# Late steps of a recurrent attention: k for the state from the near products through DRAM, and small TensorE work in two places of a step

## The chip, the cores and the metric

The kernel runs on one core of one Trainium2 chip. The metric is the device time of one execution in microseconds. Three runs of the kernel before took 628.48, 628.6 and 628.8 us, with a median of 628.6. The profile is of one execution of 628.35 us; its span, from the first to the last recorded instruction, is 626.6 us.

## The reference

Two blocks follow each other. The first is a linear attention with decay, over 4 batches, 8 heads, 768 tokens and 48 dimensions:

```python
state = zeros(B, H, D, D)
for t in range(S):
    cur = outer(u * k[t], v[t])
    y[t] = r[t] @ (state + cur)
    state = w[t][:, None] * state + outer(k[t], v[t])
```

The second takes the 3072 rows of 384 numbers that result, and computes

```python
h = x @ w_in                            # 384 -> 2048
sp = maximum(h, 0) + log1p(exp(-abs(h)))  # softplus
out = (h * erf(sp)) @ w_out             # 2048 -> 384
```

All of it is in float32 on the chip.

## The kernel before

**Tiling.** A step handles 128 tokens of two batches (`NJ` = 2), so of 16 pairs of batch and head (`NH`), which lie as 8 columns (`JP`) times two halves of the partitions (`e`). There are 12 steps, counted from 0: two groups of batches for each of six stretches of tokens. Inside a step the 128 tokens are two halves (`h`) of 64.

**The attention of a step.** The products of r and k between tokens of a half are found in six levels: at level n, blocks of 2^n tokens are cut in two, and r of the later half is multiplied with k of the earlier one, each scaled by products of w up to the cut. `scale` (line 235, VectorE) multiplies r and k in place in the tile `in`, level by level; the products of w are the totals `tot_sb` (line 287, GpSimd). The level products are the matmuls of line 423, and their results go to the tile `own` (line 442 on VectorE at level 5, line 449 on ScalarE at level 6).

From step 4 (`DIRECT`) on, only the upper levels use TensorE. The products within a block of 16 tokens (`NEAR`; 8 in step 4) are the near products: for each distance n from 0 to 15, r of a token is multiplied with k of the token n earlier (line 338), k is multiplied with one more w, so that it is carried on by one token (line 340), and the 48 products are summed (line 328). VectorE multiplies for distances 1 to 4, GpSimd for 5 to 15, VectorE sums all. The sums are rearranged from blocks to tokens by a write to DRAM (`by_blocks`) and a read (`by_tokens`), and line 375 puts them into `own`.

Then the output of the step gathers in the PSUM tile `y`: `from_own` (line 468) multiplies `own` with v in two calls, with `swap` 1 and 0; the state products (line 535) multiply r with the state at the start of each half (`S`, and `middle` for the second half). For the state itself k must have tokens on the partitions: `transpose` (line 479, eight of 128 x 128) and a copy by ScalarE to `kT` (line 483), then the matmuls of line 501, and on GpSimd and VectorE the decay and the sum (`faded` lines 485 and 517, `middle` line 513, `S_next` line 521).

**The second block.** `hidden` (line 584, 96 recorded matmuls a step) makes h, ScalarE copies it and takes softplus and erf, VectorE multiplies (line 573), and `project` (line 607, 64 recorded matmuls a step) makes the output. `hidden` runs one step after the attention, `project` three steps after it.

**Order.** The instructions of each engine stand in the order in which the program emits them (`manual_schedule`). `attend(s)` emits a step; at numbered places it calls `place(n)`, which emits pieces of the second block, in steps from 4 on by the strings of `in_order`: P is four matmuls of `project`, H six of `hidden`, A the next activation or multiplication. `attend(s)` also runs `prepare(s + 1)`, a generator that stops at each `yield`: totals, near products, the first scalings of the next step. So TensorE meets small attention work in four places of a late step, with P and H between them: level 5, behind the state products of the step before; level 6; `from_own(1)` with the transposes; the products into the state with `from_own(0)`.

**Buffers.** The tile `in` (r, k and w of a step) has two buffers. `load_step(s + 2)` is emitted behind the state products of step s, and the queue of SyncE, which issues most transfers in order, has the three transfers of `xT` (the step's output, for the second block) ahead of it. The GpSimd queue has, for a step: the totals of the next step, which wait for this load, then its near products, then `faded`.

Of the kernel before, what the change touches and what calls it, by code (L numbers as in the profile page):

```python
# [17 lines left out]
P = 128  # L18
EP = 64
HC = 64  # L20
NC = 2
NJ = 2
FG = 8
FT = 2

# [18 lines left out]
def view(ap, offset, dims):  # L44

    return bass.AP(ap.tensor, ap.offset + offset, [ap.ap[0], *dims])
# [12 lines left out]
def kernel(  # L59
# [47 lines left out]
    middles = [const.tile([P, JP, D], FP32, name=f"middle_{n}") for n in range(2)]  # L107
    faded = [const.tile([P, JP, D], FP32, name=f"faded_{n}") for n in range(NC)]
# [40 lines left out]
    def near_log(s):  # L149
        return NEAR_LOG - (s == DIRECT)  # L150
# [79 lines left out]
    def scale(s, level):  # L230

        in_t, tots = loaded[s][0], ready[s][1]
        half, nb = 1 << (level - 1), JP * C >> level
        halves = view(in_t[:, 0:2], half, [[JP * C - half, 2], [2 * half, nb], [1, half]])
        nc.vector.tensor_mul(  # L235
            halves, halves, view(tots[level - 1], 0, [[1, 2], [2, nb], [0, half]])
        )

    def prepare(s):
# [62 lines left out]
        if s == DIRECT:  # L302
            yield

        r, k, w = rows_of.pop(s)
        front = att.tile([P, 2, JP, C], FP32, name="rk1", bufs=1)
# [28 lines left out]
        def term(engine, *distances):  # L335

            for n in distances:
                engine.tensor_mul(terms[n], r[:, :, n:], k[:, :, : near - n])  # L338
                if n + 1 < near:
                    engine.tensor_mul(  # L340
                        k[:, :, : near - n - 1], k[:, :, : near - n - 1], w[:, :, n : near - 1]
                    )
# [21 lines left out]
        if near == NEAR:  # L364
            sum_up(*range(5, NEAR))
        by_blocks = dram.tile([P, NEAR, NEAR], FP32, name="by_blocks")
# [5 lines left out]
        yield  # L372
        scale(s, near_log(s))
# [9 lines left out]
    def attend(s, xT, place, behind):  # L383
# [4 lines left out]
        R, K = (in_t[:, x] for x in range(2))  # L388
        RK = in_t[:, 0:2]
        S, S_next = states[i][c % 2], states[i][1 - c % 2]  # L390
        middle = middles[s % 2]
        ends = tot.rearrange("p (n h) -> p n h", h=NC)
# [20 lines left out]
        for level in range(near_log(s) + 1 if s >= DIRECT else 1, LOG + 1):  # L413
            half = 1 << (level - 1)
            rk = made[:] if level == 1 else RK

            pp = products([P, NE, JP, HC])
            m = HC if level <= MASKED else half
            for n in range(JP):
                for s0 in range(0, C, HC):  # L420
                    for e in range(NE):
                        t0 = s0 if level <= MASKED else s0 + half
                        nc.tensor.matmul(  # L423
                            pp[s0 : s0 + m, e, n, :m],
                            lhsT=rk[rows(e), 1, n, s0 : s0 + m],
                            rhs=rk[rows(e), 0, n, t0 : t0 + m],
                            start=True,
                            stop=True,
                        )
            scale(s, level)  # L430
            keep_busy(DM, DM // 2)
            if level == 1 and s == 1:
                stay_warm()
            got = pp[:].rearrange("p e n t -> p (e n) t")
            if level == 1:
                if not s:
                    nc.vector.tensor_copy(out=first[:], in_=mask_sb[:, 0, :])
                nc.vector.tensor_mul(
                    own[:], got, first[:, None, :].to_broadcast([P, NH, HC])
                )  # L440
            elif level <= MASKED:
                nc.vector.copy_predicated(  # L442
                    rights(own[:], half),
                    rights(mask_sb[:, level - 1 : level, :].to_broadcast([P, NH, HC]), half),
                    rights(got, half),
                )
            else:
                for s0 in range(0, C, HC):
                    nc.scalar.copy(  # L449
                        own[s0 : s0 + half, :, half:], got[s0 : s0 + half, :, :half]  # L450
                    )
            if level > (NEAR_LOG if s >= DIRECT else 1):
                next(following, None)
            place(level - 1)

        def from_own(swap):  # L460
            for j in range(NJ):
                for q in range(0, NP, 2):
                    for h in range(NC):
                        e = h ^ swap
                        for p in (q, q + 1):
                            n = j * NP + p
                            t = slice(h * HC, (h + 1) * HC)
                            nc.tensor.matmul(  # L468
                                y[at(e, p), e, j, p // 2, t],
                                lhsT=vt[t, n * NE + e, :], rhs=own[t, e * JP + n, :],  # L470
                                start=swap == 1 and not j and not q, stop=True,
                                skip_group_check=True,
                            )

        last = c == n_pairs - 1
        from_own(1)
# [5 lines left out]
        kT = att.tile([P, JP, P], FP32, name="kT", bufs=1)  # L482
        nc.scalar.copy(kT[:], ps[:])
# [13 lines left out]
        for n in range(JP):  # L497
            for h in range(1 if last else NC):
                for e in range(NE):
                    t = slice(h * HC, (h + 1) * HC)  # L500
                    nc.tensor.matmul(  # L501
                        ps[h][rows(e), n, :D],
                        lhsT=kT[t, n, rows(e)],
                        rhs=vt[t, n * NE + e, :],
                        start=True,
                        stop=True,
                    )
        from_own(0)
# [7 lines left out]
        if not last:  # L516
            nc.gpsimd.tensor_mul(
                faded[1][:], middle[:], ends[:, :, 1:2].to_broadcast([P, JP, D])
            )
            for e in range(NE):  # L520
                nc.vector.tensor_add(S_next[rows(e)], faded[1][rows(e)], ps[1][rows(e), :, :D])
# [3 lines left out]

        for h, state in enumerate((S, middle)):
            if not (c or h):
                continue
            t = slice(h * HC, (h + 1) * HC)
            for j in range(NJ):  # L530
                for q in range(0, NP, 2):
                    for e in range(NE):
                        for p in (q + e, q + 1 - e):
                            n = j * NP + p
                            nc.tensor.matmul(  # L535
                                y[at(e, p), e, j, p // 2, t],
                                lhsT=state[rows(e), n, :], rhs=R[rows(e), n, t],
                                start=False, stop=True, skip_group_check=True,
                            )

        y3 = att.tile([P, UNIT], FP32, name="y3", bufs=1)
        nc.scalar.copy(y3[:].rearrange("p (j t) -> p j t", j=NJ), y[:, 1, :, 1])
        for j in range(NJ):
            nc.scalar.copy(xT[:, 0:2, j * C : (j + 1) * C], y[:, 0, j])
        nc.scalar.copy(xT[:, 2, :].rearrange("p (j t) -> p j t", j=NJ), y[:, 1, :, 0])
        for kk in range(KT):
            n = D // KT
            for e, queue in enumerate((nc.sync, nc.scalar)):
                queue.dma_start(
                    out=xT[e * EP + D : (e + 1) * EP, kk, :],  # L550
                    in_=y3[e * EP + kk * n : e * EP + (kk + 1) * n, :],
                )
# [96 lines left out]
    def in_order(s, k):  # L649


        order = ("APPPAPP", "APPPHH", "AHHH", "AHHH")
        if s == DIRECT:
            order = ("APPP", "APPP", "APPHH", "AHHH", "AHHH")
        for what in order[k]:
            if what == "A":
                advance()
            elif what == "P":
                piece(projs, s - 3)
            else:  # L660
                piece(hids, s - 1)
# [19 lines left out]
    with tc.manual_schedule(  # L681
# [5 lines left out]
        for t in (*states[0], *states[1], *middles):  # L687
            nc.gpsimd.memset(t[:], 0.0)
        nc.scalar.copy(u_row[:, :1], ident[:, :1])
# [11 lines left out]
        for s in range(n_steps):  # L701
# [8 lines left out]
            def place(n):  # L710
                if n == LOG - 1 and DIRECT - 1 <= s < n_steps - 2:
                    load_rows(s + 2)
# [15 lines left out]

            attend(s, xTs[s], place, lambda: convert_at(LOG + 2))
# [4 lines left out]
        for k in range(12):  # L734
            in_order(n_steps + k // 4, k % 4)
# [96 lines left out]
```

## Time and profile before

| | busy us | share of the span |
|---|---|---|
| TensorE (PE) | 611.9 | 98% |
| VectorE (DVE) | 402.6 | 64% |
| ScalarE (ACT) | 301.3 | 48% |
| GpSimd (POOL) | 258.0 | 41% |

| group | count | busy us |
|---|---|---|
| L584, hidden, TensorE | 1152 | 259.5 |
| L607, project, TensorE | 768 | 254.0 |
| L423, level products, TensorE, from `in` | 2368 | 38.4 |
| L479, transposes, TensorE | 96 | 13.1 |
| L483, kT copy, ScalarE | 12 | 12.2 |
| L235, scalings with totals, VectorE | 60 | 90.8 |
| L338 and L340, near terms, GpSimd, from and to `words` and `rk` | 147 | 151.9 |

The counts are recorded instructions; a wide matmul of the program stands as two. Busy time of different engines overlaps. The granted TensorE clock is 0.999 over the span.

### The profile page before, as it was taken

How to read it: one execution, taken by the hardware profiler on the slowest of the kernel's cores; microseconds unless marked ns; L12 is line 12 of the kernel's file. 1: busy time of each engine (PE TensorE's matmuls, PEld its weight loads, DVE VectorE, ACT ScalarE, POOL GpSimd, SP SyncE). 2: the span in 40 equal slices, each digit the busy share in tenths (PEclk: the TensorE clock that was granted, in tenths of full speed). 3: DMA queues.
4: the chain of work that ended last, by engine and by line, in shares of the span. 5: the costliest groups of instructions: out<-in, count | busy, mean ns of one | idle time of the engine just before them, and what ended most of it. 6: DMA issues, size and time to landing. Idle time of an engine off the chain costs nothing.

```text
span 626.6 us, 15491 instructions
## 1 busy us (share of the span) xinstructions
PE 611.9 (98%) x6886; PEld 451.0 (72%) x6886; DVE 402.6 (64%) x445; ACT 301.3 (48%) x374; POOL 258.0 (41%) x267
## 2 busy tenths in 40 slices
PE   8989999999999999999999999999999999999997
PEld 7668777578678668668668768768768768768654
DVE  5697696994597996895795796797796430020300
ACT  2547878535546534534534534534534543534600
POOL 4448184600278197096097097097087100000000
PEclk9999999999999999999999999999999999999999
DMA  8375471330320600511420421321310100000000
GB/s 330 124 267 189 182 252 56 160 110 10 134 103 9 213 29 12 175 67 18 154 82 12 157 84 18 132 103 19 115 45 10 17 14 13 7 25 1 0 26 25
DMA packets 32819, 54.83 MB, mean 88 GB/s; under 512 B 19568, under 2 KB 24944, under 8 KB 31344
## 3 DMA queue, kind: packets, MB, share of 16 engines
q1 hardware_dynamic: 31600, 53.25, 24.4%
q8 instruction: 54, 0.88, 0.6%
q10 hardware_dynamic: 1152, 0.59, 0.4%
q14 instruction: 13, 0.11, 0.1%
HBM read 46.88 MB, written 5.77 MB: 84 GB/s over the span
## 4 chain that ended last, share of the span: by engine, by line
PE 83%; DVE 8%; POOL 3%; issue 2%; ACT 2%; DMA 1%; SPq 0%; DVEq 0%; POOLq 0%; ACTq 0%
PE m L607 36%; PE m L584 34%; PE pp L423 5%; DVE in L235 3%; PE pp L479 2%; PE y L468 2%; PE y L535 2%; PE pp L501 1%; PE m L686 1%; DMA in<-in_rkw 1%; DVE sums L328 1%; POOL tot_sb L287 1%; DVE h L573 1%; DVE own L442 1%; DVE words L340 1%
## 5 line engine op out<-in xcount | busy, mean ns | idle before, releaser
L584 PE MATMUL m<-xT,w_in_sb 128*128 128x256 f32 x1152 | 259.5, 382 | 1.5 <-DVE w_in_sb L203 1.3
L607 PE MATMUL m<-w_out_sb,h 128*128 128x384 f32 x768 | 254.0, 489 | 1.3 <-POOL w_out_sb L207 1.3
L584 PEld LDWEIGHTS m<-xT,w_in_sb 128*128 128x128 f32 x1152 | 215.5, 190 | 35.2 <-issue 2.4
L607 PEld LDWEIGHTS m<-w_out_sb,h 128*128 128x128 f32 x768 | 144.0, 190 | 98.7 <-POOL w_out_sb L207 1.9
L593 ACT COPY h<-m 128x512 f32<-128x512 f32 x96 | 56.0, 583 | 133.8 <-PE m L584 133.7
L235 DVE TENSOR_TENSOR in<-in,tot_sb 128x1024 f32<-128x1024 f32 x60 | 90.8, 1514 | 41.2 <-PE pp L423 39.1
L573 DVE TENSOR_TENSOR h<-h,sp 128x1024 f32<-128x1024 f32 x48 | 70.8, 1516 | 60.7 <-ACT sp L569 60.7
L340 POOL TENSOR_TENSOR words<-words,rest 128x480 f32<-128x480 f32 (+4 forms) x70 | 72.4, 1035 | 5.5
L287 POOL TENSOR_TENSOR tot_sb<-in 128x512 f32<-128x512 f32 x12 | 15.0, 1247 | 121.3 <-DMA in<-in_rkw 121.3
L328 DVE TENSOR_REDUCE sums<-words 128x6 f32<-128x288 f32 (+8 forms) x66 | 30.4, 472 | 35.6 <-POOL words L338 35.3
L338 POOL TENSOR_TENSOR rk<-words 128x528 f32<-128x528 f32 (+3 forms) x28 | 47.9, 1712 | 6.2 <-issue 4.0
L616 ACT COPY o<-m 128x384 f32<-128x384 f32 x24 | 11.5, 478 | 79.3 <-PE m L607 79.1
L423 PEld LDWEIGHTS pp<-in 48*64 48x64 f32 (+1 forms) x2368 | 33.8, 125 | 17.4 <-issue 8.0
L566 ACT ACTIVATE sp<-h 128x2048 f32<-128x2048 f32 x24 | 45.9, 1911 | 0.3
L569 ACT ACTIVATE sp<-sp 128x2048 f32<-128x2048 f32 x24 | 45.9, 1911 | 0.3
L423 PE MATMUL pp<-in 48*64 48x64 f32 (+1 forms) x2368 | 38.4, 212 | 4.8 <-DVE in L235 2.2
L569 ACT ACT_TABLE_LOAD x24 | 30.8, 1283 | 20.5 <-issue 18.0
L287 POOL TENSOR_TENSOR tot_sb<-tot_sb 128x256 f32<-128x256 f32 (+4 forms) x60 | 35.1, 584 | 4.5
L328 DVE TENSOR_REDUCE sums<-rk 128x14 f32<-128x672 f32 (+9 forms) x54 | 34.7, 698 | 0.0
L338 POOL TENSOR_TENSOR words<-words 128x336 f32<-128x336 f32 (+6 forms) x49 | 31.6, 646 | 3.8
L566 ACT ACT_TABLE_LOAD x24 | 30.8, 1283 | 3.2 <-issue 2.8
L449 ACT COPY own<-pp 32x512 f32<-32x512 f32 x24 | 13.8, 575 | 35.5 <-PE pp L423 35.2
(67 smaller groups left out, 458.2 us busy)
## 6 DMA issues: line engine op xcount, KB each, us to landing
in<-in_rkw SPq DMA_DIRECT2D x11, 1536.0 KB, 7.0
words<-in_moe_w_in SPq DMA_DIRECT2D x8, 768.0 KB, 5.6
words<-in_moe_w_out SPq DMA_DIRECT2D x8, 768.0 KB, 4.6
words<-in_rk_rows SPq DMA_DIRECT2D x8, 768.0 KB, 8.6
v<-in_v SPq DMA_DIRECT2D x12, 384.0 KB, 7.3
out<-o SPq DMA_DIRECT2D x24, 192.0 KB, 1.9
rest<-in_w_rows SPq DMA_DIRECT2D x8, 384.0 KB, 8.7
in<-in_rkw SPq DMA_DIRECT2D x2, 512.0 KB, 4.9
```

Source lines behind the costliest of these rows:

```text
L235: nc.vector.tensor_mul(halves, halves, view(tots[level - 1], 0, [[1, 2], [2, nb], [0, half]]))
L287: nc.gpsimd.tensor_mul(new, pair[:, :, 0], pair[:, :, 1])
L328: nc.vector.tensor_reduce(out=view(sums[:], n, [[near * (NEAR + 1), NEAR // near], [NEAR + 1, near - n]]), in_=terms[n], axis=mybir.AxisLi ...
L338: engine.tensor_mul(terms[n], r[:, :, n:], k[:, :, : near - n])
L340: engine.tensor_mul(k[:, :, : near - n - 1], k[:, :, : near - n - 1], w[:, :, n : near - 1])
L423: nc.tensor.matmul(pp[s0 : s0 + m, e, n, :m], lhsT=rk[rows(e), 1, n, s0 : s0 + m], rhs=rk[rows(e), 0, n, t0 : t0 + m], start=True, stop=True,)
L566: nc.scalar.activation(held[0][:], h[:], AF.Softplus)
L569: nc.scalar.activation(held[0][:], held[0][:], AF.Erf)
L573: nc.vector.tensor_mul(h[:, part], h[:, part], held[0][:, part])
L584: nc.tensor.matmul(ps[:, ff, :], lhsT=w_in_sb[:, g * FG + f + ff, kk * P : (kk + 1) * P], rhs=xT[:, kk, :], start=kk == 0, stop=kk == KT - 1,)
L593: nc.scalar.copy(h[:, f : f + FT, :], ps[:])
L607: nc.tensor.matmul(ps[j][:], lhsT=gs[g][:, f, j * C : (j + 1) * C], rhs=w_out_sb[:, g * FG + f, :], start=g + f == 0, stop=g == NG - 1 and ...
```

## The change

From step 5 on the transposes are left out. k, which the near products carry on in place, is now carried to the end of its block of 16 (one more w per distance: `m`), so that at the end each k holds the decay from its token to the end of its block. The rows with it are written to DRAM (`k_blocks`) and read back with tokens on the partitions (`kT`). What is missing is the decay from the end of the block to the end of the half of 64: three small GpSimd operations put it together from the totals (`over_blocks`), two small matmuls turn it (`spread_blocks`), ScalarE copies it, and it goes through DRAM too, to be spread over the tokens (`g_rows`, `spread`). VectorE multiplies `kT` by it. k therefore no longer needs the scaling at level 6, and `scale` leaves it out there. The code of `attend` is split into functions, and a new `attend_late` emits steps from 5 on in another order: `from_own(1)` of the step before, level 5, `from_own(0)` and the state products of the step before stand in one place; level 6, the turning matmuls and the products into the state in the other. All P pieces stand between the first and the second, all H pieces between the second and the first of the next step. `fence`, a small VectorE copy out of `y`, stands between the two calls of `from_own`. `middle` and `faded` have one buffer each instead of two.

The purpose is to have less TensorE work that is not the two wide products, and to change between the two kinds less often.

The functions that are only moved (`level_products`, `take_level`, `from_own`, `state_part`) compute as before and are left out here.

```diff
     def scale(s, level):
...
+        n = 1 if s > DIRECT and level == LOG else 2
+        halves = view(in_t[:, 0:2], half, [[JP * C - half, n], [2 * half, nb], [1, half]])
...
+            to = over_blocks[:].rearrange("p (h b) n -> p b h n", h=NC)
+            nc.gpsimd.tensor_mul(to[:, 0], quarter, half)
+            nc.gpsimd.tensor_copy(out=to[:, 1], in_=half)
+            nc.gpsimd.tensor_copy(out=to[:, 2], in_=last)
...
                 engine.tensor_mul(terms[n], r[:, :, n:], k[:, :, : near - n])
-                if n + 1 < near:
-                    engine.tensor_mul(
-                        k[:, :, : near - n - 1], k[:, :, : near - n - 1], w[:, :, n : near - 1]
-                    )
+                m = near - n - (s == DIRECT)
+                if m:
+                    engine.tensor_mul(k[:, :, :m], k[:, :, :m], w[:, :, n : n + m])
...
         if near == NEAR:
             sum_up(*range(5, NEAR))
+            k_blocks = dram.tile([P, NEAR, D], FP32, name="k_blocks")
+            nc.sync.dma_start(out=k_blocks[:], in_=k_rows)
         by_blocks = dram.tile([P, NEAR, NEAR], FP32, name="by_blocks")
...
+            kTs[s] = att.tile([P, NH, D], FP32, name="kT", bufs=1)
+            nc.sync.dma_start(
+                out=kTs[s][:], in_=k_blocks[:].rearrange("(g b) s d -> (b s) g d", g=NH)
+            )
         scale(s, near_log(s))
...
+    def fence():
+        nc.vector.tensor_copy(
+            out=seen[:].rearrange("p (e g t) -> p e g t", e=NE, g=NP),
+            in_=y[:].rearrange("p e j q t -> p e (j q) t")[..., HC - 1 : HC + 1],
+        )
...
+    def spread_blocks(s, pp):
+        n = D // 2
+        for e in range(NE):
+            nc.tensor.matmul(
+                pp[:EP, e, 0:2, HC // 2 : HC // 2 + n],
+                lhsT=over_blocks[rows(e)].rearrange("p b n -> p (b n)"),
+                rhs=ident[rows(e), rows(e)], start=True, stop=True,
+            )
+        few = att.tile([EP, NE * 2, n], FP32, name="few", bufs=1)
+        nc.scalar.copy(
...
+        nc.sync.dma_start(
+            out=g_rows[:].rearrange("b (n d) -> (b n) d", n=JP),
...
+        nc.sync.dma_start(
+            out=spread[s][:].rearrange("p n e d -> p (n e d)"),
...
+    def attend_late(s, place):
+        c, in_t, vt, own, S, S_next, ends = parts_of(s)
+        RK = in_t[:, 0:2]
+        before = s - 1 if s - 1 > DIRECT else None
+        if before:
+            from_own(before, ready[before][0], 1)
+            fence()
+        pp = products([P, NE, JP, HC])
+        level_products(pp, RK, LOG - 1)
+        scale(s, LOG - 1)
+        take_level(own, pp, LOG - 1)
+        if before:
+            from_own(before, ready[before][0], 0)
+            through_state(before, xTs[before])
+            if s + 1 < n_steps:
+                load_step(s + 1)
+        following = prepare(s + 1) if s + 1 < n_steps else iter(())
+        kT = kTs[s]
+        nc.vector.tensor_mul(
+            kT[:].rearrange("p (e n) d -> p n e d", e=NE),
+            kT[:].rearrange("p (e n) d -> p n e d", e=NE), spread[s][:],
+        )
+        nc.gpsimd.tensor_mul(faded[0][:], S[:], ends[:, :, 0:1].to_broadcast([P, JP, D]))
+        next(following, None)
+        place(0)
+        next(following, None)
+        place(1)
+        pp = products([P, NE, JP, HC])
+        level_products(pp, RK, LOG)
+        if s + 1 < n_steps:
+            spread_blocks(s + 1, pp)
+        take_level(own, pp, LOG)
+        ps = products([P, NC, JP, HC])
+        ps = [ps[:, h] for h in range(NC)]
+        state_part(s, kT, ps)
+        scale(s, LOG)
+        for e in range(NE):
+            nc.vector.tensor_add(middle[rows(e)], faded[0][rows(e)], ps[0][rows(e), :, :D])
+        place(2)
+        next(following, None)
+        if s < n_steps - SPC:
+            nc.gpsimd.tensor_mul(
+                faded[1][:], middle[:], ends[:, :, 1:2].to_broadcast([P, JP, D])
+            )
+            for e in range(NE):
+                nc.vector.tensor_add(S_next[rows(e)], faded[1][rows(e)], ps[1][rows(e), :, :D])
+        place(3)
+        for _ in following:
+            pass
+        place(4)
...
-        order = ("APPPAPP", "APPPHH", "AHHH", "AHHH")
+        order = ("APPPAPP", "APPP", "HH", "AHHH", "AHHH", "PPAPP")
...
+        s = n_steps - 1
+        from_own(s, ready[s][0], 1)
+        fence()
+        advance()
+        piece(projs, s - 2)
+        from_own(s, ready[s][0], 0)
+        through_state(s, xTs[s])
+        in_order(s + 1, 5)
+        for k in range(1, 15):
+            in_order(s + 1 + k // 5, k % 5)
```

## The prediction

> **What bounds the kernel now.** I read the busy shares first (PE 611.9 of 626.6 us), then the chain of waits over one late step, because an average over 12 steps says nothing of the stage that is changed. In the chain below (start, duration, engine, line) each row starts where the one before ends.
>
> ```profile
> 301.65 1.04 PE y L535 x64
> 302.69 0.93 PE pp L423 x64
> 303.62 13.10 PE m L607 x40
> 316.72 0.69 PE pp L423 x50
> 317.41 7.94 PE m L607 x24
> 325.35 5.18 PE m L584 x24
> 330.52 0.59 PE y L468 x32
> 331.12 1.02 PE pp L479 x8
> 332.14 7.77 PE m L584 x36
> 339.91 0.87 PE pp L501 x64
> 340.78 0.45 PE y L468 x32
> 341.23 7.97 PE m L584 x36
> ```
>
> TensorE has no gap from one set of state products (L535) to the next: a late step is 47.55 us (302.69 to 350.24) of TensorE. So removed TensorE work is gained, as long as nothing else then becomes longer than the step.
>
> What could is the chain that prepares the next step. I took it from the timelines of GpSimd, VectorE and the DMA queue for the same step. VectorE ends it (start, duration, operation, in brackets the idle time ahead and its releaser):
>
> ```profile
> 340.14 2.85 DVE L573 TENSOR_TENSOR h<-h,sp 128x1024 f32<-128x1024 f32 x2
> 342.92 1.13 DVE L513 TENSOR_TENSOR middle<-faded,pp 48x384 f32<-48x384 f32 x2
> 344.99 1.12 DVE L521 TENSOR_TENSOR s<-faded,pp 48x384 f32<-48x384 f32 x2 [0.95 <-POOL faded L517]
> 346.14 1.23 DVE L235 TENSOR_TENSOR in<-in,tot_sb 128x1024 f32<-128x1024 f32 x1
> 347.28 1.22 DVE L375 TENSOR_TENSOR own<-block_sb,by_tokens 128x1024 f32<-128x1024 f32 x1
> 351.24 1.23 DVE L235 TENSOR_TENSOR in<-in,tot_sb 128x1024 f32<-128x1024 f32 x1 [2.74 <-PE pp L423]
> ```
>
> The scaling at 346.14 ends at 347.37; the level-5 products of the next step (L423) need it and start at 350.24. So the slack is 2.9 us of 47.55. I count this chain from E, the end of the state products (302.69): `in` is issued at 305.94, after three xT transfers that hold the DMA queue; it has landed when GpSimd starts:
>
> ```profile
> 313.18 1.04 POOL L287 TENSOR_TENSOR tot_sb<-in 128x512 f32<-128x512 f32 x1 [16.04 <-DMA in<-in_rkw]
> 314.30 2.73 POOL L287 TENSOR_TENSOR tot_sb<-tot_sb 128x256 f32<-128x256 f32 x5
> 316.99 1.33 POOL L338 TENSOR_TENSOR rk<-words 128x528 f32<-128x528 f32 x1
> ```
>
> Behind the totals in its queue stand 21 near terms, the last ending at 339.98. Over five steps (E = 255.14, 302.69, 350.24, 397.78, 445.33; last term 292.16, 339.98, 387.27, 434.42, 482.39) that end is E+37.0 in the mean, 36.6 to 37.3.
>
> **What the Trainium skill says.** "SBUF — State Buffer", section "Who interferes with whom": a VectorE instruction with two SBUF inputs and a GpSimd instruction that reads SBUF block each other for a whole instruction; reductions never do. The trace agrees: GpSimd's 480-wide term takes 1.20 us or 2.07, its faded product 0.83 or 1.81; VectorE's line 375 takes 1.22 or, beside that product, 1.86. "Trainium Architecture — The Big Picture", "Inside one NeuronCore": engines run apart and meet only in semaphores; so what counts is the order in each queue. "DMA: Bandwidth & Descriptors", "Anatomy of one DMA — SWDGE (gpsimd) path": some 2 us of a transfer are fixed, most of it the receipt of the last write. SyncE issues these here, and the trace agrees roughly: xT lands 1.8 us after issue, by_blocks 1.7, by_tokens 2.9.
>
> **The change, part by part: TensorE.** The row of the 8 transposes is 1.02 us. A run of wide products costs 215.8 ns each for L584 (20.72 us / 96 in the tail of the chain) and 322.6 for L607 (41.29 / 128). By that 36 of L584 are 7.77, as after the transposes, but 7.97 after small products; 40 and 24 of L607 are 12.90 and 7.74 against 13.10 and 7.94. So going back to wide work costs 0.20, and going into small work 0.59 - 0.45 = 0.14 (L468 after wide and after small): 0.34 for a place. The transposes pay 0.20 of that in their own row: 0.82 to 0.88 remain, I take 0.85.
> - Per late step: transposes -0.85; two places fewer -0.68; two spreading products of 48 columns +0.1 (estimate from L501's rate, between 0.03 and 0.2). TensorE's own step becomes 47.55 - 1.43 = 46.1.
> - Merging lines 535, 423 and 468 removes no product.
>
> **VectorE.** Per step: scaling at level 6 for r alone, half of 1.23; multiplying kT by the spread factors +0.95 to 1.12 (line 357 is 128x768 too); wider near terms, 192 columns, +0.2; `fence`, 128x16 out of PSUM, 0.2 (nearest 128x48 reduce 0.20; 0.1 to 0.3). VectorE is idle for about 10 us of a step, so only its place in a chain matters: the fence does stand in one.
>
> **New waits, and what is queued behind them.** `fence` waits for the own products with swap 1; behind it on VectorE stand the scaling at level 5 and the level-5 blocks, needed by level 6 some 21 us later. Multiplying kT waits for two loads; behind it stand VectorE's near terms, which GpSimd needs at E+14: some us of room. The load of kT waits on the DMA queue for the write of k_blocks, ahead of xT and `in`, but at about E+42.5, before these are due. The store of the spread factors waits for ScalarE's small copy after level 6 and holds the loads of rows for the step after next: room of half a step. Beyond the fence's own 0.2, counted below, these waits cost nothing; the work named hides them.
>
> **ScalarE.** The 1.01 us kT copy goes, a 64x96 copy comes: beside other work, 0.
>
> **DMA.** k_blocks is written and read back as kT (384 KB each way), and spread is loaded. kT is multiplied only after the fence and needed 20 us later: 0. But k_blocks is written ahead of by_blocks in one queue. by_tokens landed 4.9 us after the last term at 202.03 (by_tokens issued 204.04, + 2.9); at the 300 GB/s of the loads, k_blocks puts 1.3 on it: 6.2.
>
> **The chain, new, from E.** GpSimd: last term at 37.0; three new 16-wide operations for `over_blocks`, 0.22 + 0.08 each (48 wide is 0.29, 96 is 0.39), +0.9, ahead of the terms; k is now carried one distance further, so the widths 480..48 become 528..48, one 528 operation more, 1.33 + 0.08 = +1.4; VectorE is in contention 1 us less (half a scaling), -0.4. Last term E+38.9. Now faded[1], formerly behind middle, is the first thing behind the terms: 0.85, 39.8. S_next 1.15: 40.95. Only then h x sp, 2.85 and 0.64 for GpSimd's faded[0] beside it: 44.4. Scaling at level 4, 1.2: **45.6**; level 5 may start. own 1.15: 46.75, with by_tokens at 38.9 + 6.2 = 45.1 just in time. fence 0.2: 46.95. Behind the fence waits line 468 with swap 0 (0.45), then the state products (0.9): the next E at **48.3**.
>
> This is a loop: the state products release the buffer of the next `in`. Before, level 5 came after E, and the chain had until E+47.55. Now level 5, fence and 1.35 us of products lie ahead of the next E. The loop of 48.3 is longer than TensorE's 46.1: TensorE waits some 2.2 us in front of level 5 and swap 0, and the step is 0.75 longer than before. In step 10, without S_next, by_tokens decides: 45.1 + 1.15 + 0.2 + 1.4 = 47.85.
>
> **The sum.** Level 5 of step 5 (207.37) waits for VectorE already, behind the terms of step 4's preparation: +1.6 (1.4, and 0.2 on VectorE) = 208.97. To the next level 5: 0.16 for the cold start and 46.1 - 1.35 (the own products and state products of step 4 were earlier), then level 5 and 1.35, 2.28: E of step 5 is 256.2; the loop (206.2 + 48.3) is earlier. Four loops, steps 6 to 9: 193.2. Step 10: 47.85. E of step 10: 497.25. From level 5 of step 11 to the end the profile has 626.6 - 492.86 = 133.74; less level 5 (0.93, already done), transposes 0.85 and one place 0.35: 131.6. Span 628.85, and 2.0 between span and time (628.6 - 626.6): **630.8 us**.
>
> **Rivals.** Every us of the loop counts about five times: time = 389.35 + 5 x loop, if step 10 is 0.45 below the loop.
> - TensorE stays the bound, faster: 256.2 + 5 x 46.1 + 131.6 + 2.0 = **620.3**. For it: no gap on TensorE now, and `in` is no longer followed at once by the loads of rows, so it may land sooner than 7 us. Against: the load with no rows behind it (448.20) took 7.0 too. 2.2 us would have to vanish from the chain. Chance 0.12.
> - The loop binds, but nearer 47.3, if h x sp and faded[0] do not meet and over_blocks is cheaper: 389.35 + 236.5 = **625.9**. Chance 0.2. At 47.6 to 48.1 the time is within 0.2%.
> - by_tokens or `in` come later beside the new transfers, loop 49.0: **634.4**. Chance 0.15.
> - The forecast: 0.53.
>
> The ends of the unknown terms (fence 0.1 to 0.3, over_blocks 0.6 to 1.0, `in` at E+9.4 to 10.5, faded[0]'s 0 to 0.64) make 0.7 on the loop, 3.5 on the time; leaving out the 620 case and the far end of the slow one gives 625 to 634.5. Faster by over 0.2% (loop under 47.6): the first rival, most of the second and a little of the forecast, 0.26; within, 0.19; slower, 0.55.
>
> **What would show it.** Right: in the late steps TensorE waits 1 to 3 us for line 235's operation on VectorE or for the fence; E to E is about 48.3; the chain of waits leaves TensorE there and goes through VectorE, GpSimd and `in`; the tail after step 11's level 5 is 2 us shorter. Wrong: no wait on TensorE in steps 6 to 10 and 46.1 from E to E; or the waits there, but with the last term before E+38, so that the loop ends under 47.6; or TensorE waiting for kT ahead of the products into the state.

## The result, and the profile after

The changed kernel takes 636.85 us (median of four runs: 638.04, 638.04, 635.66, 634.01), against 628.6 before: 1.0124 times as long, with an interval of 1.0086 to 1.0163. The forecast was 630.8, with a range of 625 to 634.5: the direction is right, the rise is almost four times as large as forecast, and the time lies outside the range. The profiled run took 638.04 us with a span of 636.3; the forecast span was 628.85, so 7.45 us are to be found.

The page of the kernel after shows first that the clock is no longer full all through. The first line is the granted TensorE clock in 40 slices of 15.9 us, in tenths; the second the chain of waits by engine.

```profile
PEclk9999999999999799999999999799999999999999
PE 52%; POOL 22%; DVE 9%; DMA 8%; issue 5%; ACT 2%; SPq 1%; POOLq 0%; DVEq 0%; ACTq 0%
```

TensorE now carries 52% of the chain. Two slices have a 7: at about 207 to 223 and at about 398 to 414 us. The mean clock is 0.989 (before: 0.999). In the four runs it went with the time: 0.989 in the two of 638.04, 0.995 in the two of 635.66 and 634.01.

The chain over step 7 (start, duration, engine, line), from one set of state products (L484) to the next, shows the loop that the prediction drew:

```profile
306.88 0.94 PE y L484 x63
...
309.99 1.57 SPq L498
...
311.66 6.88 DMA in<-in_rkw
...
318.61 1.05 POOL tot_sb L293
...
323.28 1.22 POOL over_blocks L316
324.50 1.14 POOL over_blocks L317
...
347.13 0.80 POOL faded L587
...
349.11 3.00 DVE h L705 x2
352.11 1.15 DVE in L241
353.30 1.21 PE pp L424 x64
...
354.52 0.19 DVE seen L467
354.75 0.66 PE y L458 x32
355.42 0.94 PE y L484 x63
```

From E = 307.82 to 356.36 is 48.54 us; 48.3 were forecast. In words: state products, three xT transfers in the queue (L498), the load of `in`, totals, `over_blocks`, near terms to 347.13 (E+39.3), `faded`, S_next, h x sp, the scaling (to E+45.4), level 5, `fence` (L467, column `seen`), `from_own(0)`, state products. TensorE waits twice on it; the view of its waits has us in total, times, and the longest:

```profile
PE pp L424 <- DVE in L241: 6.6, 7, 2.2
PE y L458 <- DVE seen L467: 3.5, 4, 2.2
```

These are the forecast waits, but not in every step. Call the stretch from E5 to E6 step 6, and so on: the two waits together are 0.3 us in step 6, 1.8 in step 7 (1.52 and 0.29), 3.9 in step 8, nothing in step 9 and 0.8 in step 10, where 2.2 in each was forecast; one of 2.2 stands ahead of level 5 of step 5. What was not forecast at all follows some of them. The windows below have the stretch, its length, the busy times with counts of TensorE, its weight loads, VectorE, ScalarE and GpSimd, then the granted clock, the DMA share and GB/s; the second fence is TensorE's timeline of the waits there, with the wait and its releaser in brackets.

```profile
402.00:403.00 1.00, 0.98 (x64) 0.98 (x64) 0.00 (x0) 0.00 (x0) 0.00 (x0) 1.00 1.17 160
404.00:405.00 1.00, 0.00 (x0) 0.00 (x0) 1.00 (x1) 0.00 (x0) 0.00 (x0) 0.50 0.64 82
...
409.00:410.00 1.00, 1.00 (x3) 0.61 (x2) 0.97 (x2) 0.47 (x2) 0.00 (x0) 0.50 0.00 0
411.00:412.00 1.00, 1.00 (x5) 0.60 (x4) 0.96 (x2) 0.67 (x1) 0.00 (x0) 1.00 0.20 52
```

```profile
402.02 1.16 PE L424 MATMUL pp<-in 48*64 48x64 f32 x64 [1.71 <-DVE in L241]
405.39 1.11 PE L458 MATMUL y<-own,v 64*48 64x64 f32 x32 [2.21 <-DVE seen L467]
```

From 403.33 to 410.16 us, behind the wait of 1.71 us and through that of 2.21, the clock is half of the full one; such a stretch is called a spell of low clock below. The 32 products of L458 take 1.11 us instead of 0.66, the state products after them 1.71 instead of 0.94, the 64 of L739 21.8 instead of 20.84. The same happens from 208.77 to 215.60 us, behind the wait of 2.22 us in front of level 5 in step 5: level 5 takes 1.99 instead of 1.16, the 64 of L739 23.2.

In step 8 `own` starts late, and the transfers ahead of it show why (start, duration):

```profile
396.33 3.91 DMA by_blocks<-sums
400.26 3.63 DMA by_tokens<-by_blocks
403.91 1.24 DVE own L398
```

By step:

| | forecast | measured | difference | what it consists of |
|---|---|---|---|---|
| start to E5 | 256.2 | 260.7 | +4.5 | low clock 3.2; a gap of 1.03 inside the state products |
| E5 to E6 | 48.3 | 47.1 | -1.2 | `in` issued at E+2.9 and landed in 6.45 |
| E6 to E7 | 48.3 | 48.54 | +0.2 | |
| E7 to E8 | 48.3 | 51.85 | +3.55 | by_tokens late: waits 2.1 longer than in step 7; low clock 1.2 |
| E8 to E9 | 48.3 | 48.82 | +0.5 | no wait of the loop: TensorE's own 46.3, low clock 1.0, 1.5 around a gap of 1.23 |
| E9 to E10 | 47.85 | 47.3 | -0.55 | |
| E10 to the end | 131.6 | 132.0 | +0.4 | |

### The profile page after: what moved, and what is told of

Same layout as the page of the kernel before. It is cut to its first block, busy times and chain, and to the rows that moved or that the text cites. A ratio compares the mean times of both kernels' runs of the same rounds, so it can differ in the third digit from the quotient of the medians.

```text
span 636.3 us, 15558 instructions
## 1 busy us (share of the span) xinstructions
PE 610.9 (96%) x6858; PEld 451.3 (71%) x6858; DVE 397.0 (62%) x459; ACT 293.5 (46%) x374; POOL 278.6 (44%) x295
## 4 chain that ended last, share of the span: by engine, by line
PE 52%; POOL 22%; DVE 9%; DMA 8%; issue 5%; ACT 2%; SPq 1%; POOLq 0%; DVEq 0%; ACTq 0%
PE m L739 22%; PE m L716 21%; POOL words L358 8%; DMA in<-in_rkw 6%; PE pp L424 4%; POOL rk L354 4%; POOL tot_sb L293 4%; POOL words L354 3%; DVE in L241 2%; PE y L484 2%; PE y L458 1%; SPq L498 1%; DMA by_tokens<-by_blocks 1%; DMA by_blocks<-sums 1%; DVE h L705 1%
## 5 line engine op out<-in xcount | busy, mean ns | idle before, releaser
L739 PE MATMUL m<-w_out_sb,h 128*128 128x384 f32 x768 | 255.8, 493 | 1.3 <-POOL w_out_sb L212 1.3
L739 PEld LDWEIGHTS m<-w_out_sb,h 128*128 128x128 f32 x768 | 146.2, 192 | 101.9 <-issue 3.0
L241 DVE TENSOR_TENSOR in<-in,tot_sb 128x1024 f32<-128x1024 f32 (+1 forms) x60 | 83.4, 1391 | 38.4 <-PE pp L424 36.5
L705 DVE TENSOR_TENSOR h<-h,sp 128x1024 f32<-128x1024 f32 x48 | 66.3, 1423 | 52.4 <-ACT sp L701 52.2
L358 POOL TENSOR_TENSOR words<-words,rest 128x528 f32<-128x528 f32 (+10 forms) x77 | 72.5, 941 | 6.0
L748 ACT COPY o<-m 128x384 f32<-128x384 f32 x24 | 11.5, 480 | 119.3 <-PE m L739 119.3
L344 DVE TENSOR_REDUCE sums<-words 128x6 f32<-128x288 f32 (+8 forms) x66 | 30.4, 472 | 44.7 <-POOL words L354 44.3
L293 POOL TENSOR_TENSOR tot_sb<-tot_sb 128x256 f32<-128x256 f32 (+4 forms) x60 | 43.1, 718 | 4.5
L354 POOL TENSOR_TENSOR rk<-words 128x528 f32<-128x528 f32 (+3 forms) x28 | 40.5, 1446 | 4.7 <-issue 2.4
L344 DVE TENSOR_REDUCE sums<-rk 128x14 f32<-128x672 f32 (+9 forms) x54 | 35.5, 704 | 10.6 <-POOL rk L354 10.4
L354 POOL TENSOR_TENSOR words<-words 128x336 f32<-128x336 f32 (+6 forms) x49 | 30.3, 618 | 3.8
L358 DVE TENSOR_TENSOR words<-words,rest 128x576 f32<-128x576 f32 (+8 forms) x34 | 28.7, 845 | 1.2
```

Of the source, the lines that this page charges most:

```text
L241: nc.vector.tensor_mul(halves, halves, view(tots[level - 1], 0, [[1, n], [2, nb], [0, half]]))
L293: nc.gpsimd.tensor_mul(new, pair[:, :, 0], pair[:, :, 1])
L344: nc.vector.tensor_reduce(out=view(sums[:], n, [[near * (NEAR + 1), NEAR // near], [NEAR + 1, near - n]]), in_=terms[n], axis=mybir.AxisLi ...
L358: engine.tensor_mul(k[:, :, :m], k[:, :, :m], w[:, :, n : n + m])
L705: nc.vector.tensor_mul(h[:, part], h[:, part], held[0][:, part])
L739: nc.tensor.matmul(ps[j][:], lhsT=gs[g][:, f, j * C : (j + 1) * C], rhs=w_out_sb[:, g * FG + f, :], start=g + f == 0, stop=g == NG - 1 and ...
```

## The experiments

Three theories, with the numbers that the expectations use. **Theory 1**: the time is the loop of waits (load of `in`, GpSimd, VectorE, level 5, fence); shorten it and TensorE is the bound again. **Theory 2**: VectorE's queue alone makes the step longer, and the transfers have room. **Theory 3**: the loss is a lower TensorE clock that comes from the new order of the work and not from waits. Beside them stands a question on the low clock: under theories 1 and 2 it comes from TensorE's waits, so that a kernel whose TensorE doesn't wait long keeps the full clock. The experiments below are edits of the changed kernel but for e8; the 113 runs of the kernel before beside them took 626.8 to 631.0 us.

### e1: h x sp out of the chain

From step 5 on the multiplication h x sp of place 3 is emitted behind the multiplication of `kT` in the next step.

```diff
+        while put_off:
+            put_off.pop(0)()
...
-            if what == "A":
+            if what == "A" and k == 3 and DIRECT < s < n_steps:
+                put_off.append(later.pop(0)[0])
+            elif what == "A":
```

> The changed kernel with one thing moved: VectorE's multiplication h x sp of the second half of the units, 3.0 us, stands behind the multiplication of kT of the next step instead of ahead of the scaling at level 4. Theory 1 (a loop: state products, load of in, GpSimd's near terms, VectorE, level 5 and fence, state products): the scaling at level 4 comes 2.4 to 3 us sooner, so level 5 waits no longer; but by_tokens lands at E+45.5 in the changed kernel, so own and the fence stay where they are, TensorE waits 1.5 to 2 us in front of swap 0 instead, and the step stays at 48 to 48.5 us: 633 to 637 us. Theory 2 (VectorE's queue alone makes the step longer, the transfers have room): the step falls to 46.1 and the time to 622 to 626. Theory 3 (the loss is a lower TensorE clock that comes from the new order and not from waits): no change, 636.9, clock 0.99 or 0.995.

Measured: 635.25 us, 1.0114 [1.0095, 1.0132], clock 0.991: as theory 1 expects, and 9 us above the 622 to 626 of theory 2, which falls. TensorE's waits of this kernel:

```profile
PE y L458 <- DVE seen L467: 5.3, 5, 1.9
PE pp L424 <- DVE in L241: 3.1, 5, 2.2
```

The wait ahead of level 5 is gone in the late steps (6.6 to 3.1, and 2.2 of these are step 5), and the wait at the fence took its place (3.5 to 5.3). Behind the scaling in VectorE's queue stand `own`, which waits for by_tokens, and the fence: taking 3 us from one branch of the loop only brings out the other. The clock is at half for three spells of 3.4 us.

### e3 and e4: by_blocks ahead of k_blocks

e3 puts the write of k_blocks, 384 KB, behind the read of by_tokens in the queue; e4 has this and the edit of e1.

```diff
-            nc.sync.dma_start(out=k_blocks[:], in_=k_rows)
...
+        if near == NEAR:
+            nc.sync.dma_start(out=k_blocks[:], in_=k_rows)
```

> The changed kernel with by_blocks written and by_tokens read ahead of the write of k_blocks, VectorE's queue unchanged. Theory 1 (loop, with two chains that end nearly together): h x sp still stands ahead of the scaling at level 4, so own cannot start before E+45.5 whenever by_tokens lands; the steps keep their 48.3 to 48.5 us, and only the late by_tokens of step 8 (1.9 us) is saved: 632 to 636 us, nearer the changed kernel than e4. Rival (the transfers alone make the step longer): as e4 or better, 630 or less.

> e1 and, besides, by_blocks is written and by_tokens read ahead of the write of k_blocks. Theory 1: by_tokens now lands some 1.3 us sooner (E+44.2), own ends at 45.4, the fence at 45.6, the next E at 47.0: loop 47.0 to 47.3, so 1.2 to 1.5 us less in each of steps 6 to 9: 628 to 632 us; better than e1 by 3 to 6. Theory 2: the same as e1. Theory 3: no change against the changed kernel.

Measured: e3 633.7 us, 1.0085 [1.0066, 1.0104]; e4 630.05 us, 1.0036 [1.0018, 1.0055]. Both are in the ranges that theory 1 gave. In e3 by_blocks lands 1.7 us after its issue in every late step, where it took 2.3 behind k_blocks in four steps and 3.91 in step 8, and in step 8 `own` finds by_tokens there. The gains of e1 (1.6 us) and of e3 (3.2) are smaller than the spread of the runs, so neither edit alone is told from the changed kernel with certainty; both together gain 6.8 us, clear of it.

The profiles say less for e4 than its time does. From E5 to E10 the changed kernel takes 243.6 us, e1 241.5, e3 240.2 and e4 240.2 again; single steps of e4 take 46.8 to 49.4, where a loop of 47.0 to 47.3 was expected. Of the 5.3 us by which the span of e4 is shorter than that of e1, 4.0 lie ahead of E5, where e4 has no spell of low clock. In e4 the load of kT comes later, VectorE waits 1.4 to 1.7 us for it ahead of h x sp and its near terms, and GpSimd's last term ends at E+38.9 to E+40.5 instead of E+37.9 to E+39.5; `own` still waits for by_tokens. That the two edits remove two branches of the loop is therefore not shown by e4; e2, below, is the test of the loop. Waits at the fence of 5.9 us in five steps, the longest 2.9, are left in e4, and its runs show what the clock is worth: the three at a mean clock of 1.000 took 627.1, 627.5 and 628.9 us, two at 0.989 634.0 and 636.2. With one and the same kernel, then, 0.011 of mean clock goes with some 7 us.

### e2: the load of `in` ahead of the xT transfers

The load is emitted straight behind the state products, so it no longer stands in the queue behind the copies and transfers of xT. Nothing is left out.

```diff
-    def through_state(s, xT):
+    def through_state(s, xT, then=lambda: None):
...
+        then()
         y3 = att.tile([P, UNIT], FP32, name="y3", bufs=1)
...
-            through_state(before, xTs[before])
-            if s + 1 < n_steps:
-                load_step(s + 1)
+            through_state(
+                before, xTs[before], lambda: load_step(s + 1) if s + 1 < n_steps else None
+            )
```

> The changed kernel with the load of the next in issued directly behind the state products, ahead of the three xT transfers, which held it for 2.8 to 3.3 us. Theory 1 (loop): everything from the load to own comes 2.5 to 3 us sooner against E, by_tokens included; the loop falls from 48.5 to under 46, TensorE's 46.1 bounds the steps 6 to 10; the only wait left is that of level 5 in step 5 (2.2 us), with its spell of low clock (3 us): 623 to 627 us. Theory 2 (VectorE's queue): also faster, so this run does not tell 1 from 2. Theory 3 (clock from the new order): no change in clock; the steps get shorter by their waits alone, some 8 us in all, but spells of low clock stay in the late steps: 629 to 632.

Measured: 626.06 us over 20 runs, 0.9964 [0.9953, 0.9974]. This beats both kernels, lies in the range of theory 1, and is below the 629 to 632 of theory 3. `in` is issued at E+0.06 instead of E+2.9 to E+3.8. GpSimd's timeline in this kernel, E = 306.14:

```profile
313.50 1.06 POOL L293 TENSOR_TENSOR tot_sb<-in 128x512 f32<-128x512 f32 x1 [14.28 <-DMA in<-in_rkw]
...
317.46 0.24 POOL L316 TENSOR_TENSOR over_blocks<-tot_sb 128x16 f32<-128x16 f32 x1
317.65 0.20 POOL L317 COPY over_blocks<-tot_sb 128x16 f32<-128x16 f32 x1
```

It starts at E+7.4 instead of E+10.8, and the two operations that took 1.22 and 1.14 us take 0.24 and 0.20, since VectorE sums beside them (L344) where h x sp ran. The near terms behind them take 24.4 us instead of 21.4, as h x sp now runs beside those, and the last term ends at E+36.2 instead of E+39.3. In the chain, TensorE has no gap over the loop:

```profile
350.14 0.93 PE pp L424 x64
351.07 0.45 PE y L458 x32
351.52 0.90 PE y L484 x64
352.41 4.71 PE m L740 x14
```

E to E is 46.28 us (306.14, 352.42, 398.69), against 46.1 worked out for TensorE's own step. So the TensorE part of the prediction holds, and what withheld it was the loop. Ahead of these steps the kernel still waits 2.17 us (level 5 of step 5) and 1.94 (level 5 of step 6), and has a gap of 1.09 inside the state products; its clock stays full there.

### e5: filler products in place of waits

Two products of 128 x 384 whose result nothing uses ahead of level 5 in every late step, and one behind it from step 6 on; the rest is computed as in the changed kernel.

```diff
+    def fill(ps, times):
+        for _ in range(times):
+            nc.tensor.matmul(
+                ps[:, :DM], lhsT=ident[:], rhs=w_in_sb[:, 0, :], start=True, stop=True,
+            )
...
+        fill(pp[:, 0].rearrange("p n t -> p (n t)"), 2)
         level_products(pp, RK, LOG - 1)
...
+        if before:
+            fill(ps_m.tile([P, DM], FP32, name="m"), 1)
```

> The changed kernel with TensorE kept busy where it waits: in each step from 5 on, two additional products of 384 columns (0.65 us each) ahead of level 5 and one behind it, into PSUM that is not read; nothing is taken away from the waits of the chain. If the spells of low clock come from the waits (theories 1 and 2), they go, though no wait is shorter: clock 0.999, the 5 us that they cost in the profile come back, and the fillers cost about 2 us where TensorE had not waited that long (step 6, step 11): 632 to 635 us, and the runs lie closer together than 634.0 to 638.0. If they come from the order or length of the wide stretches (theory 3), the clock stays at 0.99 and the time rises to 638 to 640.

Measured: 639.3 us, 1.0176 [1.0155, 1.0198], clock 1.000 in the profile and 0.997 to 1.000 in the four runs. The waits ahead of level 5:

```profile
PE pp L424 <- DVE in L241: 2.2, 6, 0.7
```

With no wait over 0.83 us in the late steps the clock stays at 1.000 and every stretch of 64 of L748 (project in this kernel) takes 20.84 us. So the low clock comes from TensorE's waits and not from the order of the work, and theory 3 falls, though the time is the one that it gave. The time expected of the fillers did not come out: they take 1.5 us ahead of level 5 and about 1 behind it, which is more than they fill; from E6 on TensorE has no wait left and E to E is 48.9. Filling a wait that ends on another engine costs as soon as the filler outlasts it.

### e8: the new k, in the old order

The kernel before with its four places, k through DRAM instead of the transposes, and nothing of the new order or the fence; the product into the state reads `kT` as in the changed kernel, and `middle` and `faded` have one buffer each as there.

```diff
-    middles = [const.tile([P, JP, D], FP32, name=f"middle_{n}") for n in range(2)]
+    middle = const.tile([P, JP, D], FP32, name="middle")
...
+            if level == LOG and DIRECT <= s < n_steps - 1:
+                spread_blocks(s + 1, pp)
...
+            if s > DIRECT and level == LOG - 1:
+                kT = kTs[s]
+                nc.vector.tensor_mul(
+                    kT[:].rearrange("p (e n) d -> p n e d", e=NE),
+                    kT[:].rearrange("p (e n) d -> p n e d", e=NE), spread[s][:],
+                )
```

> One half of the change alone: from step 5 on k for the state comes through DRAM as in the changed kernel, but the small TensorE work stands in four places as before, level 5 behind the state products, h x sp ahead of middle, no fence. Theory 1 (the loss comes from the new order, which puts level 5, fence and 1.35 us of products into the loop): TensorE's step is 47.55 - 0.75 = 46.8; the longer GpSimd chain brings the scaling at level 4 from E+44.5 to E+46.8 or 47.5, where level 5 is due at 46.8, so waits of 0 to 0.7 us: 623.5 to 627.5 us, faster than before. Rival (the new route itself, GpSimd's 1.4 to 3 us and the transfers, is what is too long): waits of 1.5 to 2 us in each step and 630 or more.

Measured: 630.27 us over 20 runs, 1.0029 [1.0016, 1.0042]. The time expected under theory 1 (623.5 to 627.5) is missed, and the number is that of the rival, by another path than the rival's. No late step after step 5 waits ahead of level 5, as theory 1 has it, but there is a new wait:

```profile
PE pp L523 <- POOL over_blocks L318: 3.7, 5, 1.0
```

In the old order level 6 comes some 14 us after E, and the products that turn `over_blocks` stand right behind it; GpSimd has `over_blocks` only at about E+15.5. E to E is 47.8 (257.7, 305.5, 353.3): what the transposes leave free goes into this wait. So new k alone costs 1.7 us here (630.27 - 628.6), with a spell of low clock behind the wait of 2.16 us in step 5 among it, and the new order with the load where it was another 6.6 (636.85 - 630.27).

### e7, e9, e10, e11: the waits that e2 leaves

All four keep the edit of e2. e9 puts three fillers ahead of level 5 of step 5. e7 has the edits of e1 and e3 as well, and one P piece of step 5 moved ahead of its level 5. e10 moves the same P piece, and issues the load first in step 4 too; e11 adds the edit of e3 to e10. The edit of e10, but for that of e2:

```diff
+        if s == DIRECT + 1:
+            piece(projs, s - 3)
         level_products(pp, RK, LOG - 1)
...
-        through_state(s, xT)
+        through_state(s, xT, (lambda: load_step(s + 2)) if s == DIRECT else (lambda: None))
...
+        if s == DIRECT + 1:
+            order = ("APPAPP", *order[1:])
```

> e2 with three additional products of 384 columns (1.95 us, unread PSUM) ahead of level 5 of step 5 only, where e2 waits 2.2 us for VectorE: the one long wait is filled, at no cost in time, and nothing else is changed. If the spells of low clock follow long waits: clock 0.999 or above in every run, 623.5 to 625 us, and the spread of e2's runs (624.2 to 628.1) is gone above 625. If not: the same as e2, 626.1, and the same spread.

> e1, e2 and e3 together, and one piece of four products of project (2.6 us) moved from behind level 5 of step 5 to ahead of it, where TensorE waited 2.2 us. Theory 1: every late step is bound by TensorE at 46.3 us as in e2, the wait in step 5 is filled with work that has to be done anyway, no wait is longer than 1 us and the clock stays at 0.999 or above: 620.5 to 623.5 us, 2 to 4 us less than e2. Rival (the spells of low clock do not come from the waits): clock still 0.995 to 0.997 and 623 to 626.

> e2, with the load of in issued ahead of xT also behind the state products of step 4, and with one piece of four products of project (2.6 us) ahead of level 5 of step 5. h x sp stays where the changed kernel has it: in e7 its place behind kT made GpSimd's near terms end at E+40.1 against E+36.2 in e2. Theory 1: the two waits of e2 that are left (2.2 us in step 5, 1.9 in step 6) are gone, all late steps take TensorE's 46.3 us, and as no wait is over 1 us, there is no spell of low clock: 620.5 to 622.5 us, clock 0.999 or above, runs within 1.5 us of each other; below before and below e2. Rival (spells of low clock come without waits too): 622 to 626, with a spread as in e2.

> e10, and by_blocks and by_tokens ahead of k_blocks. With the loop no longer binding, by_tokens has some 2 us of room (own did not wait for it in e2), so nothing should change: within 1 us of e10. If it is slower, the later kT (its load now starts behind by_tokens) is waited for by VectorE, and then by the near terms.

Measured: e9 628.12 us, 0.9990 [0.9976, 1.0003]; e7 627.24 us, 0.9984 [0.9968, 0.9999]; e10 626.74 us, 0.9965 [0.9954, 0.9975]; e11 628.12 us, 0.9987 [0.9974, 0.9999]. None beats e2; e9, e7 and e10 miss their expected time by 3.1 to 4.2 us, and e11 is 1.4 above e10 where 1 was allowed. In e9 the first wait is filled and the one at step 6 stays (1.97 us), with a spell of low clock behind it; but its four runs at a mean clock of 1.000 also took 626.0 to 627.8 us, against 624.2 to 626.7 in e2, so the clock is not all that e9 loses. e10 shows why such edits bring nothing:

```profile
PE pp L424 <- DVE in L241: 5.0, 5, 4.0
```

The wait of 2.17 at step 5 is gone, and the one at step 6 grew from 1.94 to 4.04. It ends with the preparation of step 6, which started no earlier: its `in` was issued 2.4 us sooner (207.52 against 209.92), 1.0 us behind the load of kT, took 9.35 us instead of 6.7, and landed at 216.87 against 216.60. In e7 the last terms come at E+38.0 to E+40.1 instead of E+35.5 to E+36.2. The terms themselves take no longer (24.5 us in step 9, 24.4 in e2); what takes longer stands ahead of them. In step 9 VectorE waits 2.38 us for kT, whose load is later by the edit of e3, then has h x sp and its own near terms; beside these GpSimd's totals and `over_blocks` take 8.0 us instead of 4.7. So the 3 us taken out of one place of VectorE's queue were paid in another.

## Why the prediction was right or wrong

**Right: TensorE's own step.** 46.1 forecast, 46.28 in e2.

**Right: the loop, and what ends it; in part, its size.** 48.3 forecast, 48.54 in step 7; level 5 of step 5 at 208.97 forecast, 208.84 measured; the tail 131.6 against 132.0. The marks that would show it right came in part: the chain goes through VectorE, GpSimd and `in` in steps 6, 7 and 8, but waits of 1 to 3 us at level 5 or the fence stand only in steps 7 and 8. Steps 6 and 10 took 47.1 and 47.3, near the second rival, and in step 9 TensorE itself was the bound. e2 shows that this loop is what keeps the kernel from being faster: with the load earlier by 2.8 to 3.8 us, and nothing else changed, the late steps are those of the first rival. That rival's own argument, that `in` may land sooner than 7 us, held in four of the five steps (6.45 to 6.88 us, 7.93 in step 8). The 5.7 us by which e2 misses its 620.3 are 1.94 and 0.18 of waits and 1.09 of a gap ahead of E5, 0.9 for five loops, 0.7 around a gap of 0.42 in step 9, 0.3 each in the tail and between the profiled run and the median, and some 0.3 left.

**Right as a sum, wrong in its terms.** Some terms had errors that cancelled. `over_blocks`, 0.9 with an upper end of 1.0, took 2.48 us (323.28 to 325.76) beside h x sp. The page "SBUF — State Buffer", cited for exactly this, was applied to the wide operations only; this trace shows that a 16-wide one waits just as long. The totals took 4.67 us instead of 3.9, for the same reason, and `in` came at E+10.8 in step 7 instead of the mean of E+10.0. Against this, the contention fell on the early operations and not on the later terms, so that the last term came at E+39.3, for 38.9 forecast.

**Wrong in step 8: "by_tokens just in time".** At 6.2 us behind the last term it was to land as `own` can start. In step 8 it came 8.0 us behind (last term 395.86, `own` 403.91): by_blocks took 3.91 us to land and by_tokens 3.63, for the 1.7 and 2.9 of before. `own` waited 1.94 us, and TensorE 2.1 longer than in step 7. The third rival spoke of this, at 0.7 us in every step; it was some 2 in one. The write of k_blocks is the smaller part of the cause: ahead of by_blocks it costs 0.6 us (2.3 against 1.7 in e3), where 1.3 was forecast. The other 1.6 us of by_blocks in step 8 stays open; one such landing stands in e4 too, with k_blocks behind (3.05 us from 391.21), and one in the kernel before (2.88 from 340.25).

**Wrong, and the largest: "The sum".** It priced every wide product at its full rate and a wait at its own length, with 0.16 for a cold start, and put the clock at nothing. In this profile the low clock behind waits took 0.83 and 2.4 us in step 5, and 1.2 and 1.0 around E8: 5.4, of which some 4.4 moved E. The row from which the 0.16 comes, level 5 of step 5 behind a wait of 1.18 us, ran at full clock, so the profile of before didn't show this cost; the prediction didn't ask what the clock does after longer waits. That the low clock is tied to waiting rests on e5, which has no long wait in the late steps and keeps 1.000, and on where the low spells lie in all twelve profiles (last section). How much the clock costs is seen in e4's runs. The length of a wait alone doesn't decide: in e2's profile waits of 2.17 and 1.94 us passed at full clock, and one of 2.92 in e4's; in e9's a wait of 1.97 us brought a spell, and in e4's a wait of 0.52 and a gap of 1.13 did.

**Not in the prediction: gaps inside the state products**, 1.03 us in step 5 (259.31 to 260.34) and 1.23 in step 9 (454.92 to 456.15), charged to no engine or transfer. Gaps of 0.2 to 1.9 us stand in the state products of steps 5 or 9 in e1 to e5, e10 and e11 too, and none in e7, e8 and e9. In the changed kernel a transfer of the queue that the page calls "instruction" stands up to 2 us ahead of each (258 to 259 and 453 to 454 us), but one at 306 to 307 goes without a gap. No run was aimed at them; their cause stays open.

With these the difference closes: low clock 4.4, by_tokens 2.1 and the first gap 1.0 make 7.5 of the 7.45. That the rest comes to nothing is luck: +0.5 in step 9, +0.4 in the tail and some smaller ones stand against -1.2 in step 6 and -0.55 in step 10.

## What to carry to other kernels

Before TensorE work is removed from a step that is full, write the next step's preparation as a loop with its times; if it is longer than the shortened step, the gain turns into a wait, and moving the load at its head may be worth more than the edit itself (here 10.8 us). No run gives the earlier load to the kernel before, whose late steps have no wait that it could shorten. Price a new wait on TensorE above its length, since the products behind it may run at half clock for 3.4 us or more. Moving an operation out of a loop pays only if what it then runs beside or ahead of is not itself in the loop: h x sp was paid back at the fence in e1 and ahead of GpSimd's terms in e7.

## What the runs showed of the hardware

- In the clock records of the twelve profiles the granted clock is 1.00 or 0.50, and within a profile all its changes lie whole multiples of 3.413 us apart (in the changed kernel 208.77, 215.60, 403.33 and 410.16). Every profile can be divided at these points into stretches of 3.413 us. The seventeen stretches at full clock that stand ahead of a low spell have TensorE without a matmul for 44 to 75% of the time (1.5 us or more); of the 2143 others, up to 1 us before the end of the span, seven have 42 to 49%, and the rest less.
- So a wait brings a low clock when about half of one stretch is idle: the wait of 2.22 us in the changed kernel fell into one (63%), that of 2.17 in e2 across two (33 and 30%). This is worked out from the records and was not tested by an edit; it would also let the same kernel have different spells from run to run. Of the 113 runs of the kernel before, 21 have a mean clock of 0.994 to 0.997, and none of these was profiled.
- A low spell lasted 3.4, 6.8 or 10.2 us. One of 3.4 cost 1.8 us (e8: 40 products of L749 in 14.86 us instead of 13.10), the two of 6.8 in the changed kernel 3.2 and 2.2. The Trainium skill, "TensorE: Matmul & The Clock Gate", section "HAM oscillation — how this bites in real kernels", gives the rule that idle gaps should stay under about 3.4 us. Here a wait of 2.22 us was followed by half the clock from 208.77 to 215.60 us, so staying under that figure is not enough.
- A 16-wide GpSimd operation takes 0.20 to 0.24 us beside VectorE's sums (e2) and 1.14 to 1.22 beside a VectorE multiplication of two tiles (changed kernel), five times as long; a 480-wide one takes 1.20 or 2.07.
- A load that is issued sooner need not land sooner: issued 1.0 us behind the load of kT (384 KB in rows of 192 bytes), `in` took 9.35 us instead of 6.7 (e10 against e2).
